# Sparse attention and a spatial gMLP on one core: two heads at once on halves of the PE rows, p transposed by DMA, gMLP between attention steps

## The chip, the core and the metric

One NeuronCore of a Trainium2 chip. The metric is device time in microseconds (us) of one execution of the whole program. The names are those of the profile: PE (TensorE matmul) and PEld (its weight loads), DVE (VectorE), ACT (ScalarE), POOL (GpSimd), SP (SyncE, which here only issues DMAs). SBUF is the on-chip memory of 128 partitions, PSUM the eight banks (512 fp32 a partition each) that PE writes.

## What is computed

```
scores = 0.125 * q @ k.T                  # q, k, v: 8 batches x 8 heads x 576 x 64, fp32
keep   = scores >= rowmax(scores) - tau   # tau = 0.02
p      = where(keep, exp(scores - rowmax), 0);  attn = p / (sum(p) + 1e-9)
x      = (attn @ v), heads side by side   # 8 x 576 x 512
h      = relu(x @ w_in)                   # 512 -> 1024;  u, v = halves of 512
v_n    = (v - mean) / sqrt(var + 1e-6)    # over the 512 features
v_s    = w_spatial @ v_n + b_spatial      # 576 x 576, over the tokens
out    = (u * v_s) @ w_out                # 8 x 576 x 512
```

576 tokens are four chunks of 128 rows and one of 64.

## The kernel before

It has two stages, one after the other. Order within a stage is left to a scheduler that places the instructions of the program on each engine; buffers (`bufs` of each pool) bound how far it can run ahead.

Attention goes head by head (64 heads). SP loads q and k in ten DMAs of at most 128x64 (L80); PE transposes each piece (L82, against an fp32 identity) and ACT copies it into qT or kT, 64 partitions x 576 (L84). POOL issues the DMAs that load v and cast it to bf16 (L88); 64 columns of ones beside it (L86) make the value product give the row sums too. Then, for each of five query chunks: the fp32 score product over 64 rows of PE, 512 and 64 columns (L95), into the only score buffer (`ps_big` has `bufs=1`); row maximum on DVE (L100); the bias from it (L102); exp on ACT (L106), which gives values of at least 1 exactly where the score lies within tau of the maximum; the mask `(e >= 1) * e` on DVE into bf16 p (L109); five PE transposes of p (L114), each copied to pT by ACT (L117). After the five chunks the value product runs feature-major (L123: v is stationary, pT streams 512 and 64 columns), a reciprocal of 64x576 on DVE (L128) and a product (L131) write the head's half of xT, bf16.

The gMLP follows when all heads are done. It loads its weights (L144 to L151), transposes w_spatial on PE (L154, L156), and goes batch by batch: two products per token chunk with w_in (L171), relu on ACT (L175, L179), statistics and normalisation on DVE with a square root on ACT (L181 to L188), the spatial product (L195), the gate on DVE (L199), four PE transposes with copies (L206, L209), the product with w_out (L212), a copy (L216) and the store (L217).

Of the kernel before, what the change touches and what calls it, by code (L numbers as in the profile page):

```python
# [9 lines left out]
F32 = mybir.dt.float32  # L10
BF16 = mybir.dt.bfloat16
AX = mybir.AxisListType
ALU = mybir.AluOpType
ACT = mybir.ActivationFunctionType


@with_exitstack
def kernel(
# [11 lines left out]
):  # L30
    nc = tc.nc
    B, H, S, D = q.shape
    Dm = moe_w_in.shape[0]
    Dff = moe_w_in.shape[1]
    Dh = Dff // 2
    scale = 1.0 / math.sqrt(D)

    P = 128
    chunks = []
    o = 0  # L40
    while o < S:
        chunks.append((o, min(P, S - o)))
        o += P
    NC = len(chunks)
    fsplit = [(0, 512), (512, S - 512)] if S > 512 else [(0, S)]

    const = ctx.enter_context(tc.tile_pool(name="const", bufs=1))
    xT_pool = ctx.enter_context(tc.tile_pool(name="xT", bufs=1))

    identb = const.tile([P, P], BF16)  # L50
    make_identity(nc, identb)
    identf = const.tile([P, P], F32)
    make_identity(nc, identf)
    negtau = const.tile([P, 1], F32)
    nc.vector.memset(negtau, -float(tau))
    epsb = const.tile([P, 1], F32)
    nc.vector.memset(epsb, 1e-6)

    NF = Dm // P
    xT = [xT_pool.tile([P, B * S], BF16, name=f"xT{_}") for _ in range(NF)]  # L60

    qT_h = q.rearrange("b h s d -> b h d s")
    kT_h = k.rearrange("b h s d -> b h d s")

    taus = float(tau) * math.sqrt(D)
    with tc.tile_pool(name="qkv", bufs=3) as qkv, \
         tc.tile_pool(name="work", bufs=4) as work, \
         tc.tile_pool(name="ptbuf", bufs=2) as ptpool, \
         tc.tile_pool(name="small", bufs=6) as small, \
         tc.tile_pool(name="ps_big", bufs=1, space=bass.MemoryType.PSUM) as ps_big, \  # L70
         tc.tile_pool(name="ps_ot", bufs=1, space=bass.MemoryType.PSUM) as ps_ot, \
         tc.tile_pool(name="ps_small", bufs=2, space=bass.MemoryType.PSUM) as ps_small:
        for b in range(B):
            for h in range(H):
                qT = qkv.tile([D, S], F32)
                kT = qkv.tile([D, S], F32)
                for ci, (co, cl) in enumerate(chunks):
                    for src, dst in ((q, qT), (k, kT)):
                        ld = work.tile([P, D], F32, name="ld")
                        nc.sync.dma_start(out=ld[:cl, :], in_=src[b, h, co:co+cl, :])  # L80
                        trp = ps_small.tile([D, P], F32, name="tr")
                        nc.tensor.transpose(out=trp[:D, :cl], in_=ld[:cl, :D],  # L82
                                            identity=identf[:cl, :cl])
                        nc.scalar.copy(out=dst[:D, co:co+cl], in_=trp[:D, :cl])  # L84
                vp = qkv.tile([P, NC, 2 * D], BF16)
                nc.vector.memset(vp[:, :, D:], 1.0)  # L86
                for ci, (co, cl) in enumerate(chunks):
                    nc.gpsimd.dma_start(out=vp[:cl, ci, :D],  # L88
                                        in_=v[b, h, co : co + cl, :])

                pT = ptpool.tile([P, NC, S], BF16)
                for qi, (qo, cl) in enumerate(chunks):
                    s_ps = ps_big.tile([P, S], F32, name="sc_ps")
                    for fo, fl in fsplit:
                        nc.tensor.matmul(out=s_ps[:cl, fo : fo + fl],  # L95
# [157 lines left out]
```

## Time and profile before

| | us |
|---|---|
| median of 3 runs (2007.19 to 2008.88) | 2007.4 |
| span of the profiled execution, first to last instruction | 2006.0 |
| PE busy | 1624.4 (81%) |
| DVE busy | 937.4 (47%) |
| ACT busy | 782.2 (39%) |
| PE score products, L95 | 829.2 |
| PE transposes of p, L114 | 344.2 |
| ACT copies of p, L117 | 350.2 |
| PE value products, L123 | 197.7 |

The page gives the profiled execution no time of its own beside the span. A group row reads: line, engine, operation, out<-in with partitions x elements, count, then busy us and mean ns of one, then idle time of the engine just before and what ended it. One `matmul` of fp32 operands is two loads and two passes in the trace, so L95 counts 1280 for 640 calls. Busy times of PE are recorded with the drain of each pass, and passes overlap; distances from start to start tell what one costs in a row. In a timeline a row is start, length, engine, line, operation, shapes, count.

### The profile page before, as it was taken

The numbers are of one execution on the slowest core, as the hardware profiler recorded it, in microseconds if no ns is written. First come the engines' busy times: TensorE is split into PE (matmuls) and PEld (weight loads), VectorE is DVE, ScalarE is ACT, GpSimd is POOL, SyncE is SP. The second block draws the span as 40 slices with busy tenths as digits, with TensorE's granted clock in tenths as the row PEclk, the third lists the DMA queues.
The fourth block names the chain that finished last, engine by engine and source line by source line (L and its number), as shares of the span: only waits on it lengthen the run. The fifth ranks groups of instructions, "written<-read, shape, count | busy, mean of one in ns | idle before, by whom it ended". The sixth has DMA issues, their size and how long they took to land.

```text
span 2006.0 us, 17484 instructions
## 1 busy us (share of the span) xinstructions
PE 1624.4 (81%) x5025; PEld 631.6 (31%) x5025; DVE 937.4 (47%) x1394; ACT 782.2 (39%) x2867; POOL 177.9 (9%) x336
## 2 busy tenths in 40 slices
PE   7877888778887788878888788877888778768998
PEld 3323333333333333333333333333333333223333
DVE  3444444444434444444444444444444444444665
ACT  4333333333333333433334333333333333334444
POOL 2001110011101111011110111001111011000000
PEclk9999999999999999999999999999999999999999
DMA  2000110001100011001110011000110001003111
GB/s 33 12 13 14 15 15 10 14 14 15 15 11 14 14 15 16 10 13 15 15 15 11 13 15 15 13 12 13 15 16 13 11 14 15 4 0 69 52 65 50
DMA packets 134189, 36.44 MB, mean 18 GB/s; under 512 B 127376, under 2 KB 129488, under 8 KB 134096
## 3 DMA queue, kind: packets, MB, share of 16 engines
q1 hardware_dynamic: 89872, 28.36, 5.7%
q0 software_dynamic: 44224, 6.98, 4.6%
q8 instruction: 42, 0.69, 0.1%
q14 instruction: 51, 0.42, 0.1%
HBM read 32.79 MB, written 9.44 MB: 21 GB/s over the span
## 4 chain that ended last, share of the span: by engine, by line
PE 63%; DVE 16%; ACT 15%; issue 3%; DMA 2%; POOL 1%; ACTq 0%; POOLq 0%; DVEq 0%
PE sc_ps L95 33%; PE tr L114 11%; DVE lrec L128 10%; ACT e L106 9%; PE ot_ps L123 9%; ACT pT L117 4%; PE tr L82 3%; PE hp L171 2%; PE vs_ps L195 2%; PE op L212 2%; DVE pp L109 2%; DVE m L100 1%; DVE xT L131 1%; ACT qT L84 1%; DMA vp<-in_v_dram 1%
## 5 line engine op out<-in xcount | busy, mean ns | idle before, releaser
L95 PE MATMUL sc_ps<-kT,qT 64*128 64x512 f32 (+3 forms) x1280 | 829.2, 763 | 222.4 <-ACT e L106 221.7
L117 ACT COPY pT<-tr 128x128 bf16<-128x128 bf16 (+3 forms) x1600 | 350.2, 256 | 882.9 <-PE tr L114 875.5
L100 DVE TENSOR_REDUCE m<-sc_ps 128x1 f32<-128x576 f32 (+1 forms) x320 | 241.3, 754 | 560.4 <-PE sc_ps L95 555.5
L95 PEld LDWEIGHTS sc_ps<-kT,qT 64*128 64x128 f32 (+1 forms) x1280 | 307.1, 293 | 428.0 <-ACT e L106 322.9
L114 PE MATMUL tr<-identb,pp 128*128 128x128 bf16 (+3 forms) x1600 | 344.2, 283 | 120.1 <-DVE pp L109 62.0
L109 DVE SCALAR_TENSOR_TENSOR pp<-e 128x576 bf16<-128x576 f32 (+1 forms) x320 | 237.7, 743 | 259.0 <-ACT e L106 259.0
L114 PEld LDWEIGHTS <-pp 128*128 128x128 bf16 (+3 forms) x1600 | 148.0, 120 | 614.7 <-issue 478.9
L128 DVE RECIPROCAL lrec<-ot_ps 64x576 f32<-64x576 f32 x64 | 240.6, 3759 | 149.9 <-PE ot_ps L123 149.9
L88 POOL DMA_DIRECT2D vp<-in_v_dram x320 | 171.9, 559 | 1548.5 <-PE ot_ps L123 1543.3
L82 PE MATMUL tr<-identf,ld 128*64 128x128 f32 (+1 forms) x640 | 229.1, 398 | 16.0 <-ACT qT L84 10.1
L106 ACT ACTIVATE e<-sc_ps,bt 128x576 f32<-128x576 f32 (+1 forms) x320 | 236.6, 739 | 5.9 <-DVE bt L102 4.4
L123 PE MATMUL ot_ps<-pT,vp 128*128 128x512 bf16 (+3 forms) x640 | 197.7, 433 | 0.0
L84 ACT COPY kT<-tr 64x128 f32<-64x128 f32 (+1 forms) x320 | 79.2, 247 | 208.7 <-PE tr L82 208.5
L82 PEld LDWEIGHTS tr<-identf,ld 128*64 128x64 f32 (+1 forms) x640 | 89.8, 151 | 137.2 <-issue 53.4
L84 ACT COPY qT<-tr 64x128 f32<-64x128 f32 (+1 forms) x320 | 80.0, 250 | 10.4 <-PE tr L82 5.7
L123 PEld LDWEIGHTS <-vp 128*128 128x128 bf16 (+1 forms) x640 | 49.2, 118 | 57.9 <-issue 47.7
L195 PE MATMUL vs_ps<-vn_all,wsT 128*128 128x512 bf16 (+3 forms) x200 | 57.9, 383 | 2.0 <-DVE vn_all L188 1.1
L171 PE MATMUL hp<-w_u,xT 128*128 128x512 bf16 (+1 forms) x160 | 44.5, 394 | 11.9 <-DMA w_u<-in_moe_w_in_dram 11.9
L102 DVE TENSOR_SCALAR bt<-m 128x1 f32<-128x1 f32 (+1 forms) x320 | 44.8, 140 | 9.0
L131 DVE TENSOR_TENSOR xT<-ot_ps,lrec 64x576 bf16<-64x576 f32 x64 | 48.0, 750 | 2.0
L171 PEld LDWEIGHTS <-xT 128*128 128x128 bf16 (+1 forms) x320 | 28.7, 102 | 53.8 <-issue 29.6
L209 ACT COPY gT<-tp 128x128 bf16<-128x128 bf16 (+1 forms) x160 | 33.0, 258 | 30.5 <-PE tp L206 29.3
(35 smaller groups left out, 374.0 us busy)
## 6 DMA issues: line engine op xcount, KB each, us to landing
ld<-in_q_dram SPq DMA_DIRECT2D x256, 32.0 KB, 1.8
ld<-in_k_dram SPq DMA_DIRECT2D x256, 32.0 KB, 1.8
out_dram<-ores SPq DMA_DIRECT2D x32, 256.0 KB, 2.0
vp<-in_v_dram POOLq DMA_DIRECT2D x256, 16.0 KB, 2.1
vp<-in_v_dram POOLq DMA_DIRECT2D x64, 8.0 KB, 2.0
ld<-in_q_dram SPq DMA_DIRECT2D x64, 16.0 KB, 1.9
ld<-in_k_dram SPq DMA_DIRECT2D x64, 16.0 KB, 1.9
out_dram<-ores SPq DMA_DIRECT2D x8, 128.0 KB, 2.3
```

Of the source, the lines that this page charges most:

```text
L82: nc.tensor.transpose(out=trp[:D, :cl], in_=ld[:cl, :D], identity=identf[:cl, :cl])
L84: nc.scalar.copy(out=dst[:D, co:co+cl], in_=trp[:D, :cl])
L88: nc.gpsimd.dma_start(out=vp[:cl, ci, :D], in_=v[b, h, co : co + cl, :])
L95: nc.tensor.matmul(out=s_ps[:cl, fo : fo + fl], lhsT=qT[:D, qo : qo + cl], rhs=kT[:D, fo : fo + fl], start=True, stop=True)
L100: nc.vector.reduce_max(out=m[:cl], in_=s_ps[:cl, :], axis=AX.X)
L106: nc.scalar.activation(out=e[:cl], in_=s_ps[:cl], func=ACT.Exp, scale=scale, bias=bt[:cl])
L109: nc.vector.scalar_tensor_tensor(out=pp[:cl], in0=e[:cl], scalar=1.0, in1=e[:cl], op0=ALU.is_ge, op1=ALU.mult)
L114: nc.tensor.transpose(out=tpp[:kl, :cl], in_=pp[:cl, ko : ko + kl], identity=identb[:cl, :cl])
L117: nc.scalar.copy(out=pT[:kl, ki, qo : qo + cl], in_=tpp[:kl, :cl])
L123: nc.tensor.matmul(out=ot_ps[:, fo : fo + fl], lhsT=vp[:cl, ci, :], rhs=pT[:cl, ci, fo : fo + fl], start=(ci == 0), stop=(ci == NC - 1))
L128: nc.vector.reciprocal(out=lrec, in_=ot_ps[D:, :])
L171: nc.tensor.matmul(out=hp[:cl], lhsT=xT[f][:, rs : rs + cl], rhs=wmat[:, f, :], start=(f == 0), stop=(f == NF - 1))
```

## The change

The body is written anew, under `tc.manual_schedule()`: each engine gets its instructions in the order in which the program names them.

- Work goes by pairs of heads (32), in slots of five steps c = 0..4. Pair i has its score steps in slot i, its value product in slot i+1 (steps 3 and 4), and its q and k are transposed in slot i-1 (steps 0 to 2).
- The chunks take tokens `4p + c` for c < 4 and the last 64 tokens for c = 4. q and k of both heads are loaded side by side (128x4x2x64 and 64x2x64), so that one fp32 PE transpose serves both: head A lands in partitions 0 to 63 of qT and kT, head B in 64 to 127. The scale moves into the copy.
- A step c < 4 has three score products: A over PE rows 0 to 63, B over rows 64 to 127, each 512 columns and into banks of their own, and one over all rows against a block-diagonal tile (`kd_ring`), which gives both heads' last 64 keys. Step 4 has the block-diagonal queries (`qd_ring`) stationary and serves the last 64 queries of both heads at once. POOL writes the block-diagonal tiles.
- The maximum is one DVE instruction over both heads (1152 columns), the exps are one per head, the mask is one per step, a step later. The threshold is now exp(-tau) instead of 1.
- p goes through `dma_start_transpose` on SP: 128x1152 into nine 128x128 blocks, or 128x640 into five.
- The value product is query-major: a block of p is stationary, v with one column of ones (65 columns) streams, 25 products a head. A reciprocal of 5 columns and one product scale it; the pair's 128x640 result goes through a DMA transpose into xT.
- v is loaded as fp32 by SP and cast by POOL.
- The gMLP of batch b runs in slots 4b+5 to 4b+8, one phase a slot (`moe_v`, `moe_u`, `moe_s`, `moe_o`), one piece a step, as a filler behind the score products; its weights are loaded at the start, w_spatial transposed by DMA. u and the gate are feature-major, so the PE transposes of the gate go; the bias rides in three spare rows of the spatial product; the inverse root is a POOL power instead of a square root on ACT; the normalisation is on POOL.
- Two PSUM pools: two score buffers of three banks, two filler buffers of one.

The diff, cut to the core of what is new:

```diff
+    ptp = ctx.enter_context(tc.tile_pool(name="ptp", bufs=10))
+    ps_s = ctx.enter_context(tc.tile_pool(name="ps_s", bufs=2, space=PSUM))
+    ps_f = ctx.enter_context(tc.tile_pool(name="ps_f", bufs=2, space=PSUM))
...
+    def load(i):
...
+            for h in range(2):
+                nc.sync.dma_start(
+                    out=t[:, 0:4, h, :],
+                    in_=src[b, 2 * hp + h, 0:512, :].rearrange("(p c) d -> p c d", c=4))
...
+        nc.gpsimd.tensor_copy(out=vt[:, :, 0:4, 0:D], in_=ts[2][:, :, 0:4, :])
...
+    def load_weights():
...
+            nc.sync.dma_start_transpose(out=wsT[:, :, c * P:(c + 1) * P], in_=wsb[:, c, :])
...
+    def qk_rem(i):
...
+                nc.gpsimd.tensor_copy(out=kd_ring[i % 2][hs, hs], in_=rem[hs, 64:128])
...
+    def pv(i, h):
...
+            for c in range(5):
+                for ki in range(5):
+                    nc.tensor.matmul(out=t[:, c * 65:c * 65 + 65], lhsT=pts[i, c][:, blk, :],
+                                     rhs=vt[:, h, vb, :], start=(ki == 0), stop=(ki == 4))
...
+                nc.sync.dma_start_transpose(
+                    out=xts[b][:, hp, :].rearrange("p (c s) -> p c s", s=P),
+                    in_=xns[i].rearrange("p c d -> p (c d)"))
...
+    def moe_v(b, c):
...
+            nc.scalar.activation(out=vrel, in_=hold["t"], func=ACT.Relu)
...
+            nc.gpsimd.tensor_tensor(out=rs, in0=rs, in1=mhalf, op=ALU.pow)
...
+            nc.gpsimd.tensor_scalar(out=vn_ring[b % 2][:n, c, :], in0=vrel[:n],
+                                    scalar1=rs[:n], scalar2=nm[:n],
+                                    op0=ALU.mult, op1=ALU.add)
...
+    def step(i, c, fillers):
...
+                nc.tensor.matmul(out=s[:, 0:512], lhsT=qT[A, cs], rhs=kT[A, :],
+                                 start=True, stop=True)
+                nc.tensor.matmul(out=s[:, 1024:1536], lhsT=qT[Bh, cs], rhs=kT[Bh, :],
+                                 start=True, stop=True)
+                nc.tensor.matmul(out=view(s, 512, [[448, 2], [1, 64]]), lhsT=qT[:, cs],
+                                 rhs=kd_ring[i % 2], start=True, stop=True)
...
+        for ev in pend_ev:
+            ev()
...
+                nc.vector.tensor_reduce(out=nm, in_=both, axis=AX.X, op=ALU.max, negate=True)
...
+                    nc.scalar.activation(out=e[:, h, :], in_=both[:, h, :], func=ACT.Exp,
+                                         bias=nm[:, h:h + 1])
...
+                pt = p_ring[(pi * 4 + pc) % NP_]
+                nc.vector.scalar_tensor_tensor(out=pt, in0=pe.rearrange("p h s -> p (h s)"), scalar=ctau,
+                                               in1=pe.rearrange("p h s -> p (h s)"),
+                                               op0=ALU.is_ge, op1=ALU.mult)
+                dst = ptp.tile([P, 9, P], BF16, name="pT")
+                nc.sync.dma_start_transpose(out=dst, in_=pt)
...
+        for mm, ev in fillers:
+            mm()
+            pend_ev.append(ev)
...
+    with tc.manual_schedule():
+        load(0)
+        load(1)
+        load_weights()
+        for fl in (qk_main(0, 0), qk_main(0, 1), qk_rem(0)):
+            fl[0]()
+            fl[1]()
+        for slot in range(NPAIR + 5):
...
+                if 1 <= slot <= NPAIR and c >= 3:
+                    fillers.append(pv(slot - 1, c - 3))
+                if slot >= 5:
+                    b, ph = divmod(slot - 5, 4)
+                    fillers.append((moe_v, moe_u, moe_s, moe_o)[ph](b, c))
+                step(i, c, fillers)
+                if c == 3 and slot + 2 < NPAIR:
+                    load(slot + 2)
```

471 lines of the change are left out of this document (299 added, 172 removed).

## The prediction, made before the result was known

> **What bounds the kernel now.** I read the page first (busy times, chain), then the windows by stage, then the timeline of one query chunk.
>
> ```profile
> PE 1624.4 (81%) x5025; PEld 631.6 (31%) x5025; DVE 937.4 (47%) x1394; ACT 782.2 (39%) x2867; POOL 177.9 (9%) x336
> PE 63%; DVE 16%; ACT 15%; issue 3%; DMA 2%; POOL 1%; ACTq 0%; POOLq 0%; DVEq 0%
> PE sc_ps L95 33%; PE tr L114 11%; DVE lrec L128 10%; ACT e L106 9%; PE ot_ps L123 9%; ACT pT L117 4%; PE tr L82 3%; PE hp L171 2%; PE vs_ps L195 2%; PE op L212 2%; DVE pp L109 2%; DVE m L100 1%; DVE xT L131 1%; ACT qT L84 1%; DMA vp<-in_v_dram 1%
> 900.00:928.00 28.00, 22.48 (x67) 8.74 (x66) 12.87 (x18) 10.73 (x42) 2.69 (x5) 1.00 0.09 13
> 1830.00:2006.00 176.00, 168.03 (x803) 65.05 (x800) 109.81 (x224) 82.55 (x273) 0.00 (x0) 0.99 0.16 54
> ```
>
> The first three lines are busy time and the chain by engine and by line; the next two are windows (length, then busy us of PE, PEld, DVE, ACT, POOL, granted clock, DMA share). One head takes 28.0 us and keeps PE busy for 22.5 of them; 64 heads make about 1792 us, and the gMLP with the start some 214. Both stages run at full clock.
>
> ```profile
> 915.75 2.07 PE L95 MATMUL sc_ps<-kT,qT 64*128 64x512 f32 x2 [1.24 <-ACT e L106]
> 917.76 0.39 PE L114 MATMUL tr<-identb,pp 128*128 128x128 bf16 x2
> 918.08 0.69 PE L95 MATMUL sc_ps<-kT,qT 64*128 64x64 f32 x2
> 918.70 0.40 PE L114 MATMUL tr<-identb,pp 128*128 128x128 bf16 x2
> 918.81 0.76 DVE L100 TENSOR_REDUCE m<-sc_ps 128x1 f32<-128x576 f32 x1 [2.31 <-PE sc_ps L95]
> 919.85 0.74 ACT L106 ACTIVATE e<-sc_ps,bt 128x576 f32<-128x576 f32 x1
> 920.64 2.07 PE L95 MATMUL sc_ps<-kT,qT 64*128 64x512 f32 x2 [1.03 <-ACT e L106]
> ```
>
> This is one chunk, 4.89 us from score product to score product (915.75 to 920.64). One score buffer closes a ring: product 2.9 us, maximum, exp, and only then the next product; the transposes of p fill the gaps. So PE is nearly the bound, and a ring of latencies takes the rest. One fp32 product is two passes on PE (x2). The span is 2006.0 us; the three runs have their median at 2007.4, 1.4 above it, which I add at the end.
>
> **The change, part by part.** The unit is one slot: a pair of heads, today 2 x 28.0 = 56.0 us.
>
> **Score products.** The rows for a pass:
>
> ```profile
> 908.91 2.34 PE L95 MATMUL sc_ps<-kT,qT 64*128 64x512 f32 x4
> 909.87 0.33 PEld L95 LDWEIGHTS sc_ps<-kT,qT 64*128 64x128 f32 x1 [0.52 <-issue]
> 910.73 0.33 PEld L95 LDWEIGHTS sc_ps<-kT,qT 64*128 64x128 f32 x1 [0.52 <-issue]
> 911.04 1.03 PE L82 MATMUL tr<-identf,ld 64*64 64x64 f32 x3
> ```
>
> A load starts as the pass ahead of it starts, so a pass of 512 columns lasts 0.86 us (909.87 to 910.73), 1.67 ns a column. Two passes that stand alone between products of 128 rows take 2.01 us (915.75 to 917.76), 0.30 over 2 x 0.86: first load and change of rows. For a step c < 4 head A pays these 2.01. Head B's two passes lie on the other 64 rows, and no row of before shows two halves at work: they cost between 0 (wholly beside A's) and 1.71 us (after them). I take 0.86: passes here start in the order of the program, A's second must wait for its first on the same rows, so only B's first finds company (A's second), and B's second runs alone. Then the block-diagonal product for the last 64 keys, two passes of 128 columns: 0.43 bare, 0.83 by the 64-column pair (918.08 to 918.70, 0.62, plus 2 x 64 columns); I take 0.6. A step is 3.47 us. Step c = 4 serves both heads in 128 rows: 2.13 (908.91 to 911.04). Per slot 4 x 3.47 + 2.13 = 16.0 us, where two heads take 2 x 5 x (2.01 + 0.62) = 26.3.
>
> **q and k** transposes take whole 128-row blocks: 8 of 128 fp32 columns at 0.21, two starts of 0.15, and the 64-row rest 0.62: 2.6 us.
>
> **p, values, gMLP.**
>
> ```profile
> 1899.85 1.04 PE L171 MATMUL hp<-w_v,xT 128*128 128x512 bf16 x4
> 1900.73 0.27 PE L206 MATMUL tp<-identb,gated 128*128 128x128 bf16 x2
> 1900.84 0.81 PE L195 MATMUL vs_ps<-vn_all,wsT 128*128 128x512 bf16 x3
> L117 ACT COPY pT<-tr 128x128 bf16<-128x128 bf16 (+3 forms) x1600 | 350.2, 256 | 882.9 <-PE tr L114 875.5
> L114 PE MATMUL tr<-identb,pp 128*128 128x128 bf16 (+3 forms) x1600 | 344.2, 283 | 120.1 <-DVE pp L109 62.0
> L128 DVE RECIPROCAL lrec<-ot_ps 64x576 f32<-64x576 f32 x64 | 240.6, 3759 | 149.9 <-PE ot_ps L123 149.9
> ```
>
> The 1600 PE transposes of p (344 us of PE, overlaps counted) and their 1600 copies (350 us of ACT) go. The reciprocal of 576 columns (3.76 us a head, 10% of the chain) becomes one of 5 columns. A bf16 product of 512 columns takes 0.22 us (four from 1899.85 to 1900.73); one of 128 columns with its own weights 0.055 (two from 1900.73 to 1900.84). The query-major value product is 50 of 65 columns; bare streaming would halve the 0.055, but each has new weights, so I take 50 x 0.055 = 2.75. The gMLP per batch: 20, 16, 20 and 20 wide products in its four phases plus 16 and 20 narrow ones, 76 x 0.22 + 36 x 0.055 = 18.7 us, one phase a slot, so 4.7. Its own stage behind the attention goes.
>
> PE per slot: 16.0 + 2.6 + 2.75 + 4.7 = 26.1. To this I add what the engines' handing over costs: "issue" is 3% of the span, 60 us over 64 heads, 0.9; a slot is 27.0 us (22.3 without gMLP).
>
> **What hides.**
>
> ```profile
> L100 DVE TENSOR_REDUCE m<-sc_ps 128x1 f32<-128x576 f32 x256 | 193.4, 755 | 432.7 <-PE sc_ps L95 427.8 <-PE tr L114 3.9
> L109 DVE SCALAR_TENSOR_TENSOR pp<-e 128x576 bf16<-128x576 f32 x256 | 189.7, 741 | 171.9 <-ACT e L106 171.9
> L106 ACT ACTIVATE e<-sc_ps,bt 128x576 f32<-128x576 f32 x256 | 189.4, 740 | 5.9 <-DVE bt L102 4.4 <-ACT pT L117 0.2
> L179 ACT ACTIVATE vrel<-hp 128x512 f32<-128x512 f32 x32 | 19.0, 593 | 13.4 <-PE tp L206 7.1 <-PE hp L171 6.3
> L181 DVE BATCH_NORM_STATS2 st<-vrel 128x6 f32<-128x512 f32 x32 | 22.1, 692 | 34.6 <-ACT vrel L179 34.4
> L199 DVE SCALAR_TENSOR_TENSOR gated<-vs_ps,bsp,u_all 128x512 bf16<-128x512 f32 x32 | 23.2, 746 | 7.4 <-PE vs_ps L195 7.4
> ```
>
> DVE: 9 head-chunks' worth of maximum and of mask, at most 9 x (0.755 + 0.741) = 13.5, two value evictions under 0.8 each, gMLP 2.0 on average: 17 us. ACT: 9 exps at 0.74, three q/k copies 1.4, gMLP 2.2: 10.3 us. Both stay under 22 even in slots without gMLP. The rings are open now: two score buffers, so step c+1 waits for the exps of step c-1, which end some 3 us after that step's products (1.5 + 2 x 0.74), while PE still has a filler and a whole product before it needs them.
>
> **New waits.**
>
> ```profile
> ld<-in_q_dram SPq DMA_DIRECT2D x256, 32.0 KB, 1.8
> wld<-in_moe_w_spatial_dram POOLq DMA_DIRECT2D x4, 144.0 KB, 7.0
> q1 hardware_dynamic: 89872, 28.36, 5.7%
> 908.90 0.33 SPq L80 DMA_DIRECT2D ld<-in_k_dram  x1
> 1.36 0.29 POOL masks.py:199 TENSOR_SCALAR_AFFINE_SELECT identf<-identf 128x128 f32<-128x128 f32 x1
> ```
>
> SP now issues, per slot, four transposes of 128x1152, two of 128x640, 9 loads (0.33 us an issue, 3 us) and in one slot of four 5 stores. A transpose waits for its mask; behind it in SP's order stand the next transposes and the loads, and the value product waits for it, three steps (15 us) later. The trace has no DMA transpose. From below: 1152 pieces of 256 bytes at the 20 ns a packet of q1 (5.7% of 16 x 2006 us over 89872), on 16 engines: 1.5 us for the large one. From above: 9 blocks of 32 KB one after another at the 1.8 us of a load: 16 us. I take 2 to 4 us, near the lower row, since one issue covers all nine blocks; a slot then needs 10 to 20 us of 27, hidden. On POOL, by 0.29 us for 128 columns, v casts 2.0, diagonal copies 1.2, normalising one batch chunk 1.2 and four small operations: under 15 us in a slot; its power has no row. POOL's casts wait for their load; behind them stand the normalisations, which the gMLP needs two slots later.
>
> **The ends.** Weights move to the front. At 0.29 us for 128 columns POOL fills its constants (26 small ones, 7 us), casts v twice (4), waits for the spatial weights (7.0 by the row), reorders them (7), splits the bias (6), and only then writes the first diagonal blocks; SP stands with it, and the first p transposes behind. The first step ends after 12 us if nothing of that counted, 35 if all of it stood in a row: I take 27, since the wait runs beside fills and casts. The tail (last value product, last batch's four phases with nothing beside them) is 26 us of PE alone (18.7 and 2.75, and 4.4 for the batch before); at the present pace of 176 us for 8 batches it would be 44: I take 40.
>
> Sum: 27 + 19.5 (slot 0, no value product) + 4 x 22.3 + 27 x 27.0 + 40 = 904.7; plus 1.4, 906 us.
>
> **The rivals.**
>
> **In turn.** The halves don't run at once. Then B costs 1.71: 32 x 4 x 0.86 = 110 more, 1016 us. For it: no overlap of two products exists in the trace. Against it: only that the rows are disjoint.
>
> **Wholly at once.** 110 less, 796 us. Against it: the two passes of one product follow each other in the program. [...] No run so far shows two halves at work.
>
> **Paced by transposes.** Large one T, small ones 0.55 T: 5.1 T + 5 us per slot passes 27 from T = 4.3 us. At T = 6 a slot is 35.6, the kernel 1206.
>
> **Slower.** The transposes go block after block: 46 blocks a slot (4 x 9 + 2 x 5), each like a 32 KB load of 1.8 us (a block of 128x128 bf16 is 32 KB): 83 us a slot, 32 x 83 + 67 = 2720 us. It turns slower than before from (2006 - 67) / 32 / 46 = 1.32 us a block. For it: a load of that size does take 1.8. Against: that figure runs from issue to landing, a stretch that several transfers can share. [...]
>
> **How the numbers follow.** My case 0.48 (own range 870 to 945: ends 12 to 35 and 26 to 44, diagonal 0.43 to 0.83), halves in turn 0.22, wholly at once 0.10, pace of the transposes 0.15, block after block 0.05. From 785 to 1070 lie the first three, and the transposes' case up to T = 5; a good 0.15 is left out. A measurement of this kernel tells 0.2% from nothing (runs from 2007.19 to 2008.88). Slower 0.04 (most of the last case), same 0.01, faster 0.95.
>
> **What the profile of the changed kernel would show.** PE near 90% busy with the chain mostly on PE; a slot of 27 us; in a step, B's first pass starting with A's second, and 0.86 us later B's second; score products 16 us a slot; DVE under 17; transposes landing in under 4 us; the first value product's wait never on DMA. Wrong if the waits of the value product name a DMA, if SP is the chain, if POOL's power takes more than 4 us a chunk, or if the four passes of A and B start 0.86 us apart one after another.

## The result, and the profile after

The changed kernel takes 704.9 us (median of 4 runs, 700.8 to 706.5) where the kernel before takes 2007.7 beside it (2007.2 to 2008.9): 0.351 of its time, 95% interval 0.350 to 0.352. That is far faster, as forecast, but outside the range: 906 us was predicted, 785 to 1070. Of the runs further down, two of the four with the halves in turn were slow, 798.0 and 806.0 us, the profiled one among them, and the time given for it is that of the other two.

From the page of the changed kernel: busy time, the granted clock in 40 slices, the chain by engine, and how long the large transposes take to land.

```profile
PE 517.9 (73%) x3712; PEld 265.5 (38%) x3712; DVE 479.0 (68%) x570; ACT 299.2 (42%) x506; POOL 209.1 (30%) x497
PEclk9977777899979999899988999899997999889999
...
PE 28%; DVE 22%; DMA 14%; SPq 11%; ACT 11%; issue 8%; POOL 5%; POOLq 0%; ACTq 0%; DVEq 0%
...
pT<-p SPq DMA_TRANSPOSE x128, 3.3
```

PE is busy 73% of the span, not the forecast 90%, and the chain is spread over every engine; DMA and SP's queue together hold a quarter of it. The column of the granted clock, 0.99 throughout in the kernel before, now reads 0.7 to 0.9 and more of full.

The timeline of PE in one step of the changed kernel (start, length, line, shapes, count):

```profile
353.37 0.69 PE L368 MATMUL s<-kT,qT 64*128 64x512 f32 x1
353.38 0.69 PE L370 MATMUL s<-kT,qT 64*128 64x512 f32 x1
353.90 0.59 PE L368 MATMUL s<-kT,qT 64*128 64x512 f32 x1
353.91 0.59 PE L370 MATMUL s<-kT,qT 64*128 64x512 f32 x1
354.43 0.49 PE L372 MATMUL s<-kd,qT 128*128 128x128 f32 x2
354.76 0.80 PE L218 MATMUL f<-v,pT 128*128 128x65 bf16 x20
355.40 0.32 PE L218 MATMUL f<-v,pTr 128*128 128x65 bf16 x5
355.56 0.81 PE L343 MATMUL f<-w_o,gT 128*128 128x512 bf16 x3
```

Read the starts. Head A's first pass and head B's start 0.01 us apart, and so do their second passes: the halves of the rows do work at once, from beginning to end. The four passes take 1.06 us (353.37 to 354.43), and the step's scores 1.39 (to 354.76), where the prediction had 3.47. Not all of that comes from the halves, since one pass now takes 0.53 us where it took 0.86.

Now the same timeline just after PE has stood still for 5.6 us:

```profile
370.27 0.61 PE L248 MATMUL f<-w_in,xT 128*128 128x512 bf16 x1 [5.55 <-DMA xT<-xn]
370.81 1.22 PE L368 MATMUL s<-kT,qT 64*128 64x512 f32 x1
370.82 1.22 PE L370 MATMUL s<-kT,qT 64*128 64x512 f32 x1
371.83 1.06 PE L368 MATMUL s<-kT,qT 64*128 64x512 f32 x1
371.83 1.06 PE L370 MATMUL s<-kT,qT 64*128 64x512 f32 x1
372.82 0.80 PE L372 MATMUL s<-kd,qT 128*128 128x128 f32 x2
373.41 0.85 PE L176 MATMUL f<-identf,kn 128*128 128x128 f32 x3
```

First passes 370.81, second passes 371.83: 1.02 us apart instead of 0.53, at half the rate. A step's scores take 2.60 us here (370.81 to 373.41). So the halves at once bring the predicted 3.47 down to 2.60, and the rate brings 2.60 down to 1.39. In 102 of the 128 steps the passes are 0.53 apart; the rest run wholly or partly at half rate. Half rate is how the attention of the kernel before ran all the time: in all its 320 score products of 512 columns the two passes start 0.91 to 1.02 us apart. Its groups show the same, split by form:

```profile
L123 PE MATMUL ot_ps<-pT,vp 128*128 128x512 bf16 x256 | 149.7, 618 | 0.0
L195 PE MATMUL vs_ps<-vn_all,wsT 128*128 128x512 bf16 x128 | 35.4, 380 | 1.1 <-DVE vn_all L188 0.3
```

These are two products of the same shape and type, L123 in the attention stage and L195 in the gMLP stage: 618 against 380 ns. The granted clock in the windows of both stages reads 0.99 to 1.00, so that column did not tell them apart. The reason is in the kept trace: its first record of the clock in the kernel before, "full", is at 1820.4 us, and ahead of its first record the column reads 1.00 for want of one. At that very time the products change pace:

```profile
1817.31 1.91 PE L171 MATMUL hp<-w_u,xT 128*128 128x512 bf16 x4
1819.02 0.42 PE L154 MATMUL tp<-identb,wld 128*128 128x128 bf16 x2
1821.02 1.03 PE L171 MATMUL hp<-w_u,xT 128*128 128x512 bf16 x4
1821.99 0.38 PE L154 MATMUL tp<-identb,wld 128*128 128x128 bf16 x2
```

Four products take 1.71 us (1817.31 to 1819.02) ahead of it and 0.97 (1821.02 to 1821.99) behind it. In the changed kernel the first record is at 37.6 us; from there on the record goes between a half and full, and around the wait above it reads half from 365.2 to 375.5 us. The slices of 0.7 to 0.9 are means of the two.

Windows of the changed kernel (length, busy us of PE, PEld, DVE, ACT, POOL, granted clock, DMA share, GB/s): a slot without gMLP, one with the gMLP's first phase, one with its second.

```profile
78.50:95.50 17.00, 12.69 (x90) 7.01 (x90) 13.08 (x15) 7.48 (x12) 2.43 (x9) 0.80 0.75 142
112.50:141.30 28.80, 18.64 (x110) 8.91 (x110) 17.82 (x25) 9.69 (x17) 9.71 (x21) 0.76 0.53 93
141.30:158.10 16.80, 14.32 (x121) 7.69 (x120) 14.81 (x17) 10.25 (x18) 9.13 (x17) 1.00 0.78 138
```

At full rate (the third row, clock 1.00) a slot with gMLP keeps PE busy 14.3 us and VectorE 14.8 and takes 16.8; the slots with the first phase take 27.9 on average. From slot 5 to 31 (score products starting at 112.5 and 650.9 us) the mean is 20.7.

What PE waited for in the changed kernel (us in total, times, longest):

```profile
PE f L176 <- DMA qn<-in_q_dram: 52.0, 28, 5.0
PE f L248 <- DMA xT<-xn: 41.2, 8, 6.3
PE s L372 <- POOL kd L203: 21.6, 1, 21.6
```

The next pair's q comes late in 28 slots, the transposed attention output in all eight first phases, and once, in slot 0, the joint block of keys.

### The profile page after: what moved, and what is told of

It is laid out like the page before. It is cut to its first block, busy times and chain, and to the rows that moved or that the text cites. A ratio compares the mean times of both kernels' runs of the same rounds, so it can differ in the third digit from the quotient of the medians.

```text
span 704.7 us, 10528 instructions
## 1 busy us (share of the span) xinstructions
PE 517.9 (73%) x3712; PEld 265.5 (38%) x3712; DVE 479.0 (68%) x570; ACT 299.2 (42%) x506; POOL 209.1 (30%) x497
## 4 chain that ended last, share of the span: by engine, by line
PE 28%; DVE 22%; DMA 14%; SPq 11%; ACT 11%; issue 8%; POOL 5%; POOLq 0%; ACTq 0%; DVEq 0%
DVE negm L386 12%; PE s L368 10%; DMA qn<-in_q_dram 9%; ACT e L389 7%; DVE p L402 6%; SPq L104 5%; PE s L372 4%; DMA xT<-xn 3%; PE f L218 3%; PE f L176 3%; PE f L343 2%; PE f L282 2%; POOL vn L266 2%; SPq L406 2%; SPq L107 2%
## 5 line engine op out<-in xcount | busy, mean ns | idle before, releaser
L389 ACT ACTIVATE e<-s,negm 128x576 f32<-128x576 f32 x256 | 175.7, 738 | 284.0 <-DVE negm L386 284.0
L386 DVE TENSOR_REDUCE negm<-s 128x2 f32<-128x1152 f32 x128 | 172.8, 1350 | 114.2 <-PE s L372 113.6
L402 DVE SCALAR_TENSOR_TENSOR p<-e,ctau 128x1152 bf16<-128x1152 f32 x128 | 181.5, 1418 | 0.0
L368 PE MATMUL s<-kT,qT 64*128 64x512 f32 x256 | 163.3, 721 | 4.2 <-ACT e L389 3.8
L370 PE MATMUL s<-kT,qT 64*128 64x512 f32 x256 | 163.3, 721 | 0.0
L372 PEld LDWEIGHTS s<-kd,qT 128*128 128x128 f32 x256 | 41.4, 203 | 133.2 <-issue 107.7
L372 PE MATMUL s<-kd,qT 128*128 128x128 f32 x256 | 67.4, 348 | 21.6 <-POOL kd L203 21.6
L248 PE MATMUL f<-w_in,xT 128*128 128x512 bf16 x160 | 48.8, 427 | 41.5 <-DMA xT<-xn 41.2
L218 PE MATMUL f<-v,pT 128*128 128x65 bf16 x1280 | 51.1, 193 | 34.1 <-ACT vrel L253 12.9
L218 PEld LDWEIGHTS <-pT 128*128 128x128 bf16 x1280 | 49.6, 99 | 40.4 <-issue 34.3
L368 PEld LDWEIGHTS s<-kT,qT 64*128 64x128 f32 x256 | 42.9, 209 | 53.2 <-issue 36.9
L266 POOL TENSOR_SCALAR vn<-vrel,rs,nm 128x512 bf16<-128x512 f32 (+1 forms) x40 | 53.2, 1329 | 4.0
L370 PEld LDWEIGHTS s<-kT,qT 64*128 64x128 f32 x256 | 42.9, 209 | 0.0
L396 ACT ACTIVATE e<-s,negm 128x576 f32<-128x576 f32 x32 | 23.7, 741 | 40.6 <-DVE negm L393 40.6
```

What stands on the lines that cost most here:

```text
L218: nc.tensor.matmul(out=t[:, c * 65:c * 65 + 65], lhsT=pts[i, c][:, blk, :], rhs=vt[:, h, vb, :], start=(ki == 0), stop=(ki == 4))
L248: nc.tensor.matmul(out=t, lhsT=xts[b][:, f, c * P:(c + 1) * P], rhs=w_in[:, f, 512:1024], start=(f == 0), stop=(f == 3))
L266: nc.gpsimd.tensor_scalar(out=vn_ring[b % 2][:n, c, :], in0=vrel[:n], scalar1=rs[:n], scalar2=nm[:n], op0=ALU.mult, op1=ALU.add)
L368: nc.tensor.matmul(out=s[:, 0:512], lhsT=qT[A, cs], rhs=kT[A, :], start=True, stop=True)
L370: nc.tensor.matmul(out=s[:, 1024:1536], lhsT=qT[Bh, cs], rhs=kT[Bh, :], start=True, stop=True)
L372: nc.tensor.matmul(out=view(s, 512, [[448, 2], [1, 64]]), lhsT=qT[:, cs], rhs=kd_ring[i % 2], start=True, stop=True)
```

## The experiments

Three questions: what sets the rate of PE; what each part of the change is worth; what paces the changed kernel. Times are medians; before was near 2007.5 beside each, and a ratio is to that.

**The rate of PE.** First, zeros in the other 64 rows of the kernel before:

```
-                qT = qkv.tile([D, S], F32)
-                kT = qkv.tile([D, S], F32)
+                qT = qkv.tile([P, S], F32)
+                kT = qkv.tile([P, S], F32)
+                nc.gpsimd.memset(qT[D:, :], 0.0)
+                nc.gpsimd.memset(kT[D:, :], 0.0)
...
-                                         lhsT=qT[:D, qo : qo + cl],
-                                         rhs=kT[:D, fo : fo + fl],
+                                         lhsT=qT[:, qo : qo + cl],
+                                         rhs=kT[:, fo : fo + fl],
```

> The kernel before, with q and k transposed into the upper 64 of 128 rows and zeros in the lower 64, so that the score product fills all 128 rows of the PE array with the same columns, the same passes and the same waits (two memsets a head on POOL are added). Theory 'half rate by rows': the attention stage of before ran at half the PE rate because only half of the array worked; a 512-column fp32 pass then falls from 0.855 to about 0.43 us, PE busy per head from 22.5 to about 12 us, and the 28 us head to 20 to 24, 1500 to 1750 us in all. Rival 'half rate by gaps': the idle 5.5 us in each head keep the rate down, rows do not matter: passes stay at 0.855 and the time within 1% of 2007. Rival 'the pass simply costs this at 64 rows and half of it in the changed kernel for another reason': also no change here.

1918.0 us, ratio 0.955 (0.954 to 0.957). Its page, clock slices and the 512-column group:

```profile
PEclk8555555556565656555656565656656565659999
...
L97 PE MATMUL sc_ps<-kT,qT 128*128 128x512 f32 x512 | 476.3, 1029 | 173.4 <-ACT e L108 152.8 <-issue 19.3 <-POOL kT L78 0.9
```

Rows matter, for the same columns became faster by having zeros beside them (1029 ns a pass in the mean, 1130 in the kernel before). But the rate is up only part of the time (the clock reads 0.5 to 0.6), so the gain, 89 us, is about a quarter of what was expected: full rows in the score products alone do not hold the full rate while PE also waits for the exps (152.8 us ahead of these products). In this run the trace has records of the clock from 17.1 us on, and the column does show the half rate.

Second, extra work. Eight products behind each score product of the kernel before, once over 128 rows, once over 64:

```
+                    for _ in range(8):
+                        nc.tensor.matmul(out=dps, lhsT=identb, rhs=dum, start=True, stop=True)
                     m = small.tile([P, 1], F32, name="m")
```
```
-                        nc.tensor.matmul(out=dps, lhsT=identb, rhs=dum, start=True, stop=True)
+                        nc.tensor.matmul(out=dps, lhsT=identb[:D], rhs=dum[:D], start=True, stop=True)
```

> The kernel before, with eight extra bf16 products of 128 rows and 512 columns into an unused bank behind each score product (40 a head, results unread; the two banks of the transposes of q and k become four quarters of one). Work is only added. Theory 'half rate by gaps' (and by rows as well, since these fill all rows): the PE is now hardly ever idle, a 512-column fp32 pass falls to 0.43 us, and 40 extra products at 0.216 us (8.6 us a head) beside 22.5 / 2 = 11.3 us of own work come to about 20 us a head plus what waits remain: 1350 to 1800 us, faster than 2007 with more work. Rival 'the pass has a fixed price': 40 x 0.43 = 17 us a head are added, of which at most the 5.5 us of idle time hide some: 28 + 11.6 = 39.6 us a head, about 2650 us.

> The kernel before with the same eight extra products behind each score product as in the run with 128 rows of extra work (which came to 1773 us), but these use only 64 rows of the array, as the scores themselves do. The PE is as busy in time. Theory 'the rate follows the share of time in which the PE works': as there, 1773 us within 2%, a 512-column fp32 pass at 0.43 us. Theory 'the rate follows how many rows work': the PE stays at half rate, 40 extra products at 0.43 us = 17.1 us a head are added to 28 us of which 5.5 were idle: 39.6 us a head, 2700 to 2780 us.

With 128 rows: 1773.3 us, ratio 0.883 (0.882 to 0.885), faster with 2560 products more. With 64 rows: 2830.2 us, ratio 1.409 (1.407 to 1.412). A window in the attention, and the groups of the added and the score products, for 128 rows:

```profile
800.00:856.00 56.00, 55.53 (x267) 23.25 (x271) 29.55 (x45) 27.02 (x100) 5.45 (x11) 1.00 0.11 16
...
L107 PE MATMUL dps<-dum,identb 128*128 128x512 bf16 x2451 | 695.3, 382 | 5.9 <-issue 2.9 <-POOL identb masks.py:199 1.5
L102 PE MATMUL sc_ps<-kT,qT 64*128 64x512 f32 x512 | 322.4, 713 | 26.5 <-ACT e L116 25.5
```

and the same for 64 rows:

```profile
800.00:856.00 56.00, 56.00 (x144) 18.64 (x142) 15.20 (x22) 14.19 (x50) 2.69 (x5) 1.00 0.05 7
...
L107 PE MATMUL dps<-dum,identb 64*128 64x512 bf16 x2560 | 1292.4, 621 | 1.5 <-POOL identb masks.py:199 1.5
L102 PE MATMUL sc_ps<-kT,qT 64*128 64x512 f32 x512 | 495.5, 1070 | 25.4 <-ACT e L116 25.4
```

Both windows show PE busy from end to end. Yet the added products take 382 ns over 128 rows and 621 over 64, and the score products, untouched, 713 and 1070. The granted clock of 1.00 is a record in the first run (full from 7.3 us on); in the second the first record is at 2641.8 us, so that 1.00 says nothing.

The run with 128 rows holds the comparison within itself, too. Nothing reads the added products, and the scheduler ran them ahead of their place: the last starts at 1283.7 us, with some 300 us of attention to go. From 1287.3 to 1587.7 us the record reads half, and the same score products, first from 800 to 1080 us, then from 1290 to 1560, are

```profile
L102 PE MATMUL sc_ps<-kT,qT 64*128 64x512 f32 x96 | 53.9, 641 | 0.3
L102 PE MATMUL sc_ps<-kT,qT 64*128 64x512 f32 x74 | 76.6, 1137 | 24.5 <-ACT e L116 24.5
```

The 713 above is a mean over both. In the second stretch PE also waits again (24.5 us ahead of these products), so it does not part rows from waits; the run with 64 rows does. With PE busy for 55.53 and 56.00 of 56 us, the share of time in which it works does not set the rates of these two runs apart, 382 and 621 ns; how many rows work does. PE's busy time in all these runs also holds transposes, most of them over 128 rows (L82 and L114 of the kernel before, 573 of 1624 us); how far those count was not tried.

The records of the clock agree with the durations: in the changed kernel the two passes of a score product start 0.53 us apart in all 100 steps in which both start under a record of full, and 1.01 to 1.02 in the 18 in which both start under one of a half. What misled in the kernel before was a stretch without any.

**What each part is worth.** The two halves one after the other, by the order alone:

```
                 nc.tensor.matmul(out=s[:, 0:512], lhsT=qT[A, cs], rhs=kT[A, :],
                                  start=True, stop=True)
-                nc.tensor.matmul(out=s[:, 1024:1536], lhsT=qT[Bh, cs], rhs=kT[Bh, :],
-                                 start=True, stop=True)
                 nc.tensor.matmul(out=view(s, 512, [[448, 2], [1, 64]]), lhsT=qT[:, cs],
                                  rhs=kd_ring[i % 2], start=True, stop=True)
+                nc.tensor.matmul(out=s[:, 1024:1536], lhsT=qT[Bh, cs], rhs=kT[Bh, :],
+                                 start=True, stop=True)
```

> The kernel after, with one order swapped: the product of the joint 64 + 64 columns, which uses all 128 rows, is issued between the products of the two heads, so that the second head's product cannot start beside the first one's. All else is the same. Theory 'PE has slack': loads on SP and VectorE pace the slots, so the 0.86 us that each of 128 steps gains at full rate (110 us) is hidden for the larger part: 705 to 750 us. Rival 'PE paces the slots': 705 + 110 = 815 us, and more where the clock is at half. Forecast 745.

786.0 us (782.8 and 789.2), 81 more. The timeline of PE in this run shows B's passes (L372 here) behind the joint product, and the step 4.42 us long:

```profile
182.78 1.12 PE L368 MATMUL s<-kT,qT 64*128 64x512 f32 x2
183.83 0.49 PE L370 MATMUL s<-kd,qT 128*128 128x128 f32 x2
184.25 1.12 PE L372 MATMUL s<-kT,qT 64*128 64x512 f32 x2
...
187.20 1.12 PE L368 MATMUL s<-kT,qT 64*128 64x512 f32 x2
```

The forecast for this run, 745 with PE in hand, missed; the rival said 815, and the time lies between, nearer to the rival. By these rows A's two passes alone take 1.05 us (182.78 to 183.83); B's, once beside them, now add about as much to each of 128 steps, some 130 us, and 81 show. So PE's work is on the path for some six tenths of it, even with PE busy 73% of the time. I read this as PE meeting the waits for loads in its own order, so that much of what is added comes on top of them; no run tests that reading.

The gMLP at the end:

```
-        for slot in range(NPAIR + 5):
+        for slot in range(NPAIR + 1 + NPAIR):
...
-                if slot >= 5:
-                    b, ph = divmod(slot - 5, 4)
+                if slot > NPAIR:
+                    b, ph = divmod(slot - NPAIR - 1, 4)
```

(xtp takes 8 buffers and mw 1.)

> The kernel after, with the whole gMLP behind the last attention step instead of between the steps (eight buffers for the transposed attention output, one for u and the gated product). Theory 'weaving hides the gMLP for the larger part': attention slots go at the 16.9 us that the slots without gMLP show (36 + 31 x 16.9 = 560 us from the start), then eight batches of 23 to 28 us follow: 750 to 790 us, so the weaving is worth 45 to 85 us. Rival 'weaving gives back what it hides': the 28 us slots of the first phase, with their transposed load behind nine loads on SP and the PE at half clock after the stall, eat it up: 690 to 715. Second rival 'the gMLP products keep the PE at full rate': without them the attention slots lose the full clock and take 19 us or more: 830 and up.

769.2 us (766.7 to 769.5), 64 more, as expected. A window in its attention:

```profile
300.00:342.00 42.00, 29.84 (x191) 15.78 (x188) 30.74 (x34) 17.64 (x28) 4.84 (x18) 0.78 0.72 144
```

Its slots take 16.9 to 17.2 us each, at a clock of 0.78 in this window. The third alternative, slots of 19 us and more without the gMLP's products, did not come: the slots without gMLP take 16.7 to 17.0 in the changed kernel too.

Both undone at once:

> The kernel after with both parts undone at once: the joint product between the two heads' products, and the whole gMLP behind the last attention step. One alone cost 89 us, the other 64; if they only add up, 705 + 153 = 858. Theory 'it is the rows at work together that bring the full rate, from either part': with neither, only 64 rows work in most of the attention's PE time, the rate falls to a half as in the kernel before, and a slot needs 2 x (5.1 + 3.4 + 1.0 + 1.1 + 1.5) = 24 us: 36 + 31 x 24 + 200 = 980, 930 to 1030 us. Rival 'the denser order alone keeps the full rate': 840 to 870.

866.5 us (862.9 to 870.1), 162 more, against 81 + 64 = 145 if the two simply add. A window in its attention:

```profile
300.00:342.00 42.00, 38.24 (x182) 17.25 (x181) 27.24 (x30) 16.68 (x27) 6.14 (x19) 0.77 0.66 127
```

The theory that the rate then falls to a half throughout (980 us) is wrong. From slot 5 to slot 31 the granted clock is 0.91 in the changed kernel, 0.90 with the halves in turn, 0.80 with the gMLP at the end and 0.72 with both undone. So the gMLP between the steps holds up the rate, the halves at once only where the gMLP is at the end, and neither is needed to come well above a half. What does the rest is not taken apart further: also new are a joint product over all 128 rows for the last keys, transposes of q and k over 128 columns where they had 64, and another pattern of waits.

p transposed on PE again, as in the kernel before but eight blocks to a bank:

```
-                nc.sync.dma_start_transpose(out=dst, in_=pt)
+                pend_tr.append((dst, pt, 9))
...
+                    nc.tensor.transpose(out=t[:, j * P:(j + 1) * P],
+                                        in_=pt[:, (lo + j) * P:(lo + j + 1) * P], identity=identb)
+                nc.scalar.copy(out=dst[:, lo:lo + m, :],
+                               in_=t[:, 0:m * P].rearrange("p (k s) -> p k s", s=P))
```

> The kernel after, with the transposes of p put back on the PE (bf16 against the identity, eight blocks to a bank, copied out by ScalarE in the next step), all else as after. It adds 41 blocks a slot at 0.056 to 0.11 us = 2.3 to 4.5 us of PE and about 6 us of ScalarE (10.3 to 16 us), and takes 6.5 us of issue and all waits for masks off SP. Theory 'the DMA transposes take PE work off the path': 705 + 32 x 3.4 = 815, less the 52 us of late q loads, which no longer stand behind waiting transposes: 765. Rival 'the PE has room': 650 to 700, faster than with the DMA. Rival 'ScalarE paces with 16 us and its own waits': 830 and up.

750.3 us (746.0 to 752.2), 45 more, near the first theory's 765. The chain by engine and the group of the copies:

```profile
PE 59%; ACT 22%; DVE 7%; POOL 4%; issue 3%; DMA 3%; SPq 2%; POOLq 0%; DVEq 0%; ACTq 0%
...
L393 ACT COPY pT<-f 128x1024 bf16<-128x1024 bf16 (+1 forms) x256 | 151.1, 642 | 138.2 <-PE f L390 137.7
```

DMA and SP all but leave the chain, PE takes 59% of it: this comes near the kernel that the prediction described. The DMA transposes free PE and ScalarE (28% and 11% of the chain in the changed kernel, 59% and 22% here), and cost the queue that the loads share (11% of the chain there, 2% here). With the transposes on PE the granted clock is 0.99 over the run, against 0.91 in the changed kernel, so the 45 us are probably what is left of a larger saving; no run tests that.

**What paces the changed kernel.** SP's queue in one slot:

```profile
238.14 1.28 SPq L406 DMA_TRANSPOSE pT<-p  x1
239.47 1.30 SPq L104 DMA_DIRECT2D qn<-in_q_dram  x2
240.82 0.63 SPq L107 DMA_DIRECT2D qn<-in_q_dram  x1
```

An issue of a transpose takes 1.2 to 1.3 us, of a load 0.6, and all stand in one order behind waits for masks (69 waits of the large transposes for p, 154.5 us in total). Per slot that is 4 x 1.3 + 2 x 1.25 + 9 x 0.63 = 13.4 us. Loading earlier in the slot, then also the gMLP two steps later:

```
-                if c == 3 and slot + 2 < NPAIR:
+                if c == 0 and slot + 2 < NPAIR:
```
```
-                if slot >= 5:
-                    b, ph = divmod(slot - 5, 4)
-                    fillers.append((moe_v, moe_u, moe_s, moe_o)[ph](b, c))
+                g = (slot - 5) * 5 + c - 2
+                if 0 <= g < 20 * B:
+                    b, ph = divmod(g // 5, 4)
+                    fillers.append((moe_v, moe_u, moe_s, moe_o)[ph](b, g % 5))
```

> The kernel after, with the loads of the pair after next issued behind a slot's first step instead of its fourth (one number changed). Theory 'late loads': the PE waits 52 us in 28 slots for q (issued on SP behind three transposes that wait for masks, 1.4 steps before its use), and 41 us in eight slots for the transposed attention output that stands behind nine loads on the same queue; both shrink: slots without gMLP from 16.9 to 15.2 (VectorE's 15 us), the slots of the first phase from 27.9 to 23, 620 to 655 us in all. Rival 'VectorE paces': the wait is taken over at once by the next late thing, 690 to 705. Rival 'SP is full': nine loads of 0.6 us now stand ahead of the transposes of p, which come late for the value product: 705 or more.

> As the kernel with the earlier loads, and the whole gMLP two steps later (one slot more at the end for its last two steps), so that its first product isn't issued in the very step in which the transpose that feeds it is issued. Theory 'the first-phase slots wait for that transpose, then run at half clock': they fall to 18 to 20 us and the time by another 20 to 35 us against the earlier loads alone, to 595 to 630. Rival 'GpSimd paces that phase' (five times 0.55 + 1.33 us and the small ones, ahead of the copies of the next pair): they stay over 22 us and the time within 10 us.

647.9 us (646.8 to 648.8), as the first theory had it, and 634.2 (631.8 to 637.1), just above its forecast of 595 to 630. PE's longest wait with the earlier loads:

```profile
PE s L372 <- POOL kd L203: 30.1, 10, 20.4
```

The wait for q falls from 52.0 us to 4.4 and the first-phase slots fall from 27.9 to 23.7; with the shift they are 18.3, but the second phase rises from 16.4 to 20.3, so only 14 of the expected 20 to 35 us come. What grew is the wait for GpSimd's joint blocks: from 21.6 us in one step to 30.1 in 10, and 45.0 in 12 with the shift; 20 to 23 of each is one wait in slot 0. GpSimd, in order too, stood waiting for v. Casting v later:

```
+                if c == 4 and slot + 2 < NPAIR:
+                    cast_v(slot + 2)
```

> The kernel with the earlier loads and the gMLP two steps later (634 us), with the casts of v on GpSimd issued behind the fifth step instead of together with the loads. Theory 'GpSimd stands still for v': its in-order queue waits about 7 us a slot for v's load (last of nine on SP) and holds the normalisations and the copies of the next pair's joint blocks behind it; first and second phase (18.3 and 20.3 us) fall to 16 to 17, in all 634 - 8 x 5 = 590 to 605. Rival 'the normalisations themselves pace' (five times about 3.5 us of GpSimd in a slot): within 10 us of 634.

621.4 us (619.9 to 623.5). The cast's group and what ended GpSimd's idle time ahead of it, first with the casts beside the loads, then late:

```profile
L121 POOL CAST v<-vl 128x512 bf16<-128x512 f32 x32 | 32.2, 1008 | 233.1 <-DMA vl<-in_v_dram 206.8
```
```profile
L124 POOL CAST v<-vl 128x512 bf16<-128x512 f32 x32 | 32.6, 1019 | 26.3 <-DMA vl<-in_v_dram 24.7
```

Idle time ahead of the casts falls from 233 to 26 us, but a third of the expected 29 to 44 us is all that the kernel gains, since the second phase stays at 20.0: neither theory had its size.

A first attempt to join these with two more edits, the weights spread over slots 1 to 4 and the normalisation on ScalarE:

```
-            nc.gpsimd.tensor_scalar(out=vn_ring[b % 2][:n, c, :], in0=vrel[:n],
-                                    scalar1=rs[:n], scalar2=nm[:n],
-                                    op0=ALU.mult, op1=ALU.add)
+            nc.scalar.activation(out=vn_ring[b % 2][:n, c, :], in_=vrel[:n],
+                                 func=ACT.Identity, scale=rs[:n], bias=nm[:n])
```

> The kernel with the earlier loads and the gMLP two steps later, and besides: the first pair's q and k are made before the weights are prepared, and the weights' casts, transposes and bias rows are spread over slots 1 to 4 (the 36 us of slot 0 wait for copies on GpSimd behind those casts); the normalisation (1.33 us each on GpSimd) is done by ScalarE. Theory 'VectorE's 15 us is the next bound': slot 0 at 22, the others at 15.5 to 17, then the tail of 50: 8 + 22 + 31 x 16.3 + 45 = 580, 550 to 610. Rival 'the half clock stays in the gaps, PE work of 13.5 us at full rate is 17 or more at the mean rate': slots of 17.5 and over, 620 and up.

732.6 us (731.8 to 734.2): worse than the changed kernel itself and far from the first theory; it lies in the open range of the rival (620 and up), but for a cause that neither names. ScalarE's longest wait in this run:

```profile
ACT vn L274 <- POOL nm L271: 175.3, 40, 7.9
```

The instruction is cheap on ScalarE (0.81 us against 1.33), but it now waits there, 40 times 4.4 us, for two small results of GpSimd, whose own queue stands waiting for v (the casts are beside the loads in this version); and behind it in ScalarE's order stand the exps. The next run takes that edit back and has the late casts; the two were not tried apart.

> As the kernel with the late casts of v, and the weights' preparation spread over slots 1 to 4 behind the first pair's q and k. Slot 0 falls from 36 to about 14 us (it did in the run that had this besides the normalisation on ScalarE), slots 1 to 3 take up to 5 us more together than before: a further 15 to 20 us, 570 to 590. Rival 'the weights only move': slots 1 to 3 give it back, within 5 us of the kernel with late casts.

618.8 us (615.6 to 621.5), 2.6 less than with late casts alone, so the rival held: slot 0 falls from 35.1 to 18.6 us, slots 1 to 4 give most of it back (62.8 to 74.0). In this kernel, too, the halves in turn:

> As the kernel before this one in the list, with the joint product between the two heads' products, so that the second head's can't start beside the first one's. Where the waits for loads are gone, theory 'VectorE paces (15 us a slot)' has 2 us of room on the PE (13.5 us at full rate): 3.4 us are added and 1 to 2 of them show, + 30 to 60 us. Rival 'PE paces in any case': + 90 to 110 us, as in the changed kernel itself (+ 89).

680.2 us (677.4 to 683.8), 61 more, just past the upper end of the first theory's 30 to 60, below the rival's 90. Last, five buffers of p instead of three (`NP_ = 5`):

> The kernel with the late casts and the spread weights (619 us), with five buffers for p ahead of its transposes instead of three. VectorE waits 25.2 us there for the transposes to give a buffer back; if VectorE paces, up to that much is gained: 595 to 610. Rival 'the ring of PE, VectorE and ScalarE paces, and that wait falls into slots in which the weights are prepared and something else is late': 610 to 620.

610.0 us (608.4 to 612.8), ratio 0.304 (0.303 to 0.305), and 0.865 of the changed kernel: the fastest here, on the border of the two ranges: of the 25.2 us that VectorE waited, 8.8 came off the time. Two of its slots:

```profile
151.60:167.20 15.60, 14.67 (x126) 7.82 (x125) 15.02 (x18) 8.42 (x15) 3.81 (x9) 1.00 0.84 151
185.00:204.70 19.70, 16.47 (x111) 7.96 (x110) 16.41 (x21) 10.52 (x18) 13.93 (x28) 0.91 0.81 150
```

Where no load is late, a slot of 15.6 us has VectorE busy for 15.0 and PE for 14.7, so both are close to being the bound. The second row is a slot with the second phase, which still takes 19.7; what holds it was not tried.

## Why the prediction was wrong

By stretch, predicted and measured: to the score products of slot 1, 46.5 and 44.8 us; four slots without gMLP, 89.2 and 67.7; 26 slots with it, 702.0 and 538.4; the last slot and the tail, 67.0 and 53.8. The sums are 904.7 and 704.7. Of the 200 us, 185 lie in the slots. The start agrees by luck: its first step ends at 32.9 us where 27 was taken, and the rest of slot 0 takes 11.9 where the sum has 19.5.

**"Both stages run at full clock."** This is the step that failed first. It rested on the granted clock of 1.00 and 0.99 in two windows, and the first of them lies where the trace has no record of the clock; the attention stage ran at half rate, as 618 against 380 ns for one shape shows. Every PE term read from that stage was near twice too dear. The prediction even had both figures within reach: it priced the gMLP from its own stage at 0.22 us a product (which held) and the rest from rows at half rate. At full rate, with the halves at once and a cheaper value product, the sum of 26.1 us of PE a slot became 14.3.

**"Only B's first pass finds company."** Wrong as well. The passes of A and B start together, both of them: the order in the trace is A's first, B's first, A's second, B's second, though the program names A's whole product first. Taking 0.86 off each step gives the rival "wholly at once", 796 us, the right mechanism at a chance of 0.10; still 91 too slow, because that case used the half rate too. Four passes take 1.06 us, where the run in turn needs 1.05 for two. What the halves are worth in time is 81 us here, 61 in the better kernel.

**"A slot is 27.0 us", PE near 90% busy, the chain mostly PE.** Two errors cancelled in part. PE needs half of that, and what then comes late was not priced: q's loads and the transpose into xT behind nine loads. These waits, and the half rate that follows the long ones, put 3 to 4 us on a common slot (17.5 to 18.5 on average by phase) and 13 to 14 on one with the first phase (27.9), which brings 14.3 to a mean of 20.7. At the end of each of the seven waits for xT of 4.0 us and longer the record of the clock reads half. With the issues on SP at 0.33 us (the row of before) nine loads are 3 us; they take 5.7, and the transposes' issues, 1.3 us each, had no term. "The first value product's wait never on DMA" held but for one wait of 1.3 us, while other products waited on DMA for 52.0 and 41.2 us. In the sum itself, the 0.9 us for handing over is the share of one head, and a slot holds two; that alone would have made it some 30 us longer.

**Value product**, 2.75 us: the 25 products of a head take 0.80 (354.76 to 355.56), 1.6 a slot, or 0.032 each; by the 0.22 us of 512 columns 65 would take 0.028, so new weights each time add little. **DMA transposes**, 2 to 4 us: 3.3, in the middle, and "paced by transposes" and "block after block" are ruled out by it: nine blocks land in 3.3 us, 0.37 each, and to put them on PE costs 45 us. **VectorE under 17**: 14.8, and in the fastest version it and PE are both close to the slot's length. **GpSimd under 15 us a slot**: 9.7 and 9.1 in the rows above; its busy time was right, and its order is what cost.

What is shown and what is not: that rows at work set the rate of a busy PE is shown by the pair of runs with the same extra work on 128 and on 64 rows (382 and 621 ns); that full rows do not suffice where PE waits, by the run with zeros (the clock at 0.5 to 0.6). Which of the new products lift the rate in the changed kernel stays open, beyond the 0.72 that is left without the halves at once and the gMLP between the steps.

## What to carry to other kernels

Before a stage is priced, compare one shape in it with the same shape in another stage, or work out us per column from start to start: here a granted clock of 1.00 stood beside products of 618 ns instead of 380, where the trace had no record of the clock yet, and 2560 products more, over 128 rows, took 234 us off the kernel. When PE's work shrinks, price next what was hidden under it, queue by queue: every issue on SP with its own length (1.3 us a transpose and 0.6 a load here), and every instruction that waits at the head of an in-order queue (the casts of v, 233 us) with all that stands behind it. An instruction moved to an engine with free time is no gain if it takes its wait along, as the normalisation on ScalarE showed, 40 waits of 4.4 us.

## What the runs showed of the hardware

- PE stayed at half rate through 56.00 of 56 busy us with 64 rows at work in the score and the added products, and ran at full rate with 128 rows in the added ones: 621 and 382 ns for the same 512 columns. Around a wait of 5.6 us the changed kernel fell to half rate as well: the record reads half from 365.2 to 375.5 us, and the passes behind the wait start 1.02 us apart instead of 0.53.
- Where a trace has records of the clock, they agree with the durations: in the kernel before, four products take 1.71 us just ahead of the first record at 1820.4 us and 0.97 just behind it.
- Two fp32 products on separate halves of the rows start 0.01 us apart and keep pace in both passes.
- A product of 65 columns with new weights each time costs 0.032 us from start to start at full rate (25 in 0.80).
- To issue a DMA transpose takes SP 1.2 to 1.3 us, a load 0.6 in the changed kernel and 0.33 in the row of the kernel before that the prediction shows.
